# Attention and two expert layers in one kernel: the first float64 weights loaded and decoded in the attention's written order

## The chip, the cores and the metric

The kernel runs on one NeuronCore of a Trainium2 chip: TensorE (matmuls and transposes, called PE in the profile), VectorE (DVE), ScalarE (ACT), GpSimd (POOL) and SyncE (SP, which here only issues transfers) run their own instruction streams and wait for one another by semaphores. The metric is the device time of one execution in microseconds (us).

## The reference

Three parts follow one another. All inputs but the first layer's two weight matrices are float32.

```python
# attention: batch 2, 8 heads, 576 positions, head size 64
q_rot, k_rot = rotate(q), rotate(k)
scores = scale * q_rot @ k_rot.T
attn = exp(scores - max); attn /= sum(attn) + 1e-9
x = (attn @ v) as [1152 tokens, 512]
# first layer: w_in [512, 2048] and w_out [2048, 512] are float64
h = x @ w_in
g = max(h, 0) + log1p(exp(-abs(h)))
x = g @ w_out
# second layer: 8 experts (512 x 1024 x 512); tokens with x @ w_skip > 0 go
# to the expert of the largest logit, weighted by its probability
out = x; out[chosen] += gate * (max(x @ w1[e], 0) @ w2[e])
```

## The kernel before, in words

**Attention.** The work is cut into 40 units: for each batch b and each pair of heads hp five units of query rows, four of 128 rows (for both heads) and one called "m", which holds the last 64 rows of both heads. `Attention.run` goes through the units, i = 0 to 39 and four more steps to finish. In each step it emits instructions in the order that the list `ORDER` gives (line 26): `S0`, `S1` are the scores of the two heads on TensorE (`s_mm`), `M0`, `M1` their row maxima on VectorE (line 249), `E0`, `E1` the exponentials on ScalarE (line 262); `T0` to `T2` are the transposes of the unit before on TensorE (line 331) and `H0` to `H2` the copies of these to SBUF on ScalarE or VectorE (lines 84 and 86). `J` are the value matmuls and `N` the scaling, `Q` prepares the next pair: transposes of rotated queries and keys (`tq`), last keys and queries of all pairs (`tr`, once for each batch), loads, and rotations on GpSimd. `L` calls `do_later`, which takes the low parts that were put off, and issues the transfers that stack keys and queries into both halves of the partitions (`stack`, on SP).

A block `manual_schedule` fixes the order on TensorE, VectorE, ScalarE and SP within one step. What stands outside such a block is placed by a list scheduler, which issues an instruction when its model of the engines finds it ready; `issue_after(x)` adds that an instruction on x's engine is queued behind x.

**Float32 in two halves.** TensorE multiplies rounded float32 (fp32r). A tensor is therefore held as a high part (rounded by a ScalarE copy) and a low part (the rest, a VectorE subtraction), and three products are summed. `halves` emits the high part and returns the low part as a function to be called later.

**First pair.** There is no time to stack, so its scores use keys `kT` and queries `qT` directly with 64 rows. The last 64 keys (positions 512 to 575) of all four pairs are transposed at once by `tr`, rounded into a tile `kr`, and copied from there into the pair's `kT` by `kr_in`.

**Filler matmuls.** `warm(part)` issues `WARM[part]` matmuls on a tile of zeros, at six places of the start: 0 ahead of everything, 1 and 2 behind the first transposes of queries and keys, 3 behind `tr`, 4 behind the first unit's scores, 5 behind unit 1.

**First layer.** `Moe1` takes the hidden dimension in 16 blocks f of 128. A block has two weight halves, (f, 0) of `w_in` and (f, 1) of `w_out`, 512 KB of float64 each. `weights` loads a half on SP as int64 into one of two buffers `raw`, decodes it to float32 by three VectorE integer instructions (lines 540 to 542) into one of two buffers `wt`, rounds it on ScalarE (line 544) and takes the low part on VectorE (line 545). The tokens come in four phases; phase 0 (blocks 0 to 5, the first 512 tokens) begins at the seam with the attention. A step is `hidden` (12 matmuls for these tokens and block, line 557, then softplus on ScalarE and VectorE) and, two steps later, `out_mm` (line 595).

The halves (0, 0), (0, 1), (1, 0), (1, 1) are given out at units 29, 31, 33 and 35 (`W_AT`) by the function `side`, which is called behind the unit's manual block: the load is queued behind the last stack copy so far, the VectorE instructions behind the last maximum so far, and the list scheduler places the rest. The halves (2, 0) and (3, 0) are the first of phase 0's own, outside the attention's loop.

Of the kernel before, what the change touches and what calls it, by code (L numbers as in the profile page):

```python
# [25 lines left out]
ORDER = "S0 R T0 M0 H0 E0 S1 T1 M1 L E1 H1 J T2 N H2 Q".split()  # L26
# [5 lines left out]
W_AT = (29, 31, 33, 35)  # L32

WARM = (18, 4, 4, 3, 3, 3)
# [13 lines left out]
class Attention:  # L48
# [133 lines left out]
    def tr(self, b):  # L182
# [18 lines left out]
    def stack(self, dst, src):  # L201
        for a in range(2):
            r = slice(64 * a, 64 * a + 64)
            for o in range(2):
                d = slice(64 * o, 64 * o + 64)
                self.copied = self.nc.sync.dma_start(dst(a, d).bitcast(F32), src(a, o, r).bitcast(F32))
# [104 lines left out]
    def t_steps(self, b, hp, u):  # L311
# [18 lines left out]
        def tr(ps, i, src):  # L330
            nc.tensor.transpose(ps[:, 128 * i : 128 * i + 128], src, ident)  # L331
# [75 lines left out]
    def run(self, side=None):  # L407
        nc = self.nc
# [6 lines left out]
        with self.tc.manual_schedule(engines=self.engines):  # L415
# [17 lines left out]
        for i in range(n + 4):  # L433
# [4 lines left out]
            with self.tc.manual_schedule(engines=self.engines):  # L438
                for step in ORDER:
# [25 lines left out]
                    elif step == "L":  # L465
                        self.do_later()
# [9 lines left out]
            if side:  # L476
                side(i)
# [32 lines left out]
class Moe1:  # L510
# [4 lines left out]
    def __init__(self, nc, w_in, w_out, xh, xl):  # L515
        self.nc, self.w_in, self.w_out, self.xh, self.xl = nc, w_in, w_out, xh, xl
        self.w = {}

    def weights(self, f, wp, st, bufs, parts=(0, 1), after=nullcontext):
# [4 lines left out]
        w = self.w[f]  # L524
        fs = slice(128 * f, 128 * f + 128)
        for i in parts:
            raw = st.tile([128, 512], mybir.dt.int64, name=f"raw{f}{i}", tag="st", bufs=2)
            if i == 0:
                nc.sync.dma_start(
                    raw.rearrange("p (k n) -> p k n", k=4), self.w_in[:, fs].rearrange("(k p) n -> p k n", p=128)  # L530
                )
            else:
                nc.sync.dma_start(raw, self.w_out[fs, :])
            u = raw.bitcast(U32)
# [699 lines left out]
```

## Time and profile before

| | |
|---|---|
| median of 3 runs | 535.49 us (534.54 to 537.21) |
| profiled execution | 536.5 us |
| its span, first to last instruction | 534.7 us |
| TensorE matmuls busy | 494.9 us (93%) |
| VectorE busy | 396.2 us (74%) |
| ScalarE busy | 342.7 us (64%) |
| GpSimd busy | 121.1 us (23%) |
| mean granted TensorE clock | 0.988 of 2.4 GHz |

The profile is of one execution; times count from its first instruction. A line such as `L557 PE MATMUL h<-xh,w ... x464 | 105.2, 309 | 2.7 <-ACT w L544 1.7` is a group: line of the kernel, engine, operation, output and inputs with their shapes, how many, busy us and mean ns of one, and the engine's idle time just before them with what ended it. In the timeline `x4` means that four instructions of one kind run in one row, and `SPq` is the issue of a transfer on SP. PEld is the loading of the stationary operand. The clock that the chip granted TensorE is 1.00 at 2.4 GHz and 0.50 at 1.2 GHz; a mean between stands for a stretch with both.

### The profile page before, as it was taken

The numbers are of one execution on the slowest core, as the hardware profiler recorded it, in microseconds if no ns is written. First come the engines' busy times: TensorE is split into PE (matmuls) and PEld (weight loads), VectorE is DVE, ScalarE is ACT, GpSimd is POOL, SyncE is SP. The second block draws the span as 40 slices with busy tenths as digits, with TensorE's granted clock in tenths as the row PEclk, the third lists the DMA queues.
The fourth block names the chain that finished last, engine by engine and source line by source line (L and its number), as shares of the span: only waits on it lengthen the run. The fifth ranks groups of instructions, "written<-read, shape, count | busy, mean of one in ns | idle before, by whom it ended". The sixth has DMA issues, their size and how long they took to land. (4 is left out here: it accounts for less than half of the span.)

```text
span 534.7 us, 8595 instructions
## 1 busy us (share of the span) xinstructions
PE 494.9 (93%) x2894; PEld 397.6 (74%) x2895; DVE 396.2 (74%) x734; ACT 342.7 (64%) x770; POOL 121.1 (23%) x165
## 2 busy tenths in 40 slices
PE   7889999998879978999999999999989899999994
PEld 3667677776656656889999998998967577777773
DVE  7467687766679389699999885437875678797883
ACT  2456665665656474897677776766863487676781
POOL 0848675745113210000000000001100502221112
PEclk9899999999899999999999999999998999999998
DMA  7176547446453115134343440502333705597101
GB/s 170 51 189 159 121 122 185 108 107 170 98 157 110 51 40 156 41 119 118 120 119 118 119 119 1 198 0 83 102 118 121 266 13 191 188 364 272 54 21 37
DMA packets 41604, 65.47 MB, mean 122 GB/s; under 512 B 9184, under 2 KB 23776, under 8 KB 41552
## 3 DMA queue, kind: packets, MB, share of 16 engines
q1 hardware_dynamic: 37776, 57.89, 37.2%
q0 software_dynamic: 1440, 4.20, 2.1%
q10 hardware_dynamic: 2336, 2.74, 1.6%
q8 instruction: 26, 0.43, 0.4%
q14 instruction: 26, 0.21, 0.1%
HBM read 67.30 MB, written 7.15 MB: 139 GB/s over the span
## 5 line engine op out<-in xcount | busy, mean ns | idle before, releaser
L557 PE MATMUL h<-xh,w 128*128 128x320 f32 (+2 forms) x464 | 105.2, 309 | 2.7 <-ACT w L544 1.7
L595 PE MATMUL acc<-w,gh 128*128 128x512 f32 x288 | 78.3, 398 | 6.1 <-ACT gh L585 6.1
L557 PEld LDWEIGHTS h<-xh,w 128*128 128x128 f32 x464 | 78.1, 188 | 6.6 <-ACT w L544 2.1
L816 DVE TENSOR_TENSOR ws<-raw,ws 128x1024 fp32r<-128x1024 f32 x59 | 70.0, 1220 | 10.2 <-ACT ws L814 9.9
L557 PE MATMUL h<-xl,w 128*128 128x320 f32 (+2 forms) x232 | 69.7, 308 | 0.0
L249 DVE TENSOR_REDUCE m<-s 128x1 f32<-128x576 f32 x64 | 48.0, 753 | 25.8 <-PE s L240 20.0
L595 PEld LDWEIGHTS acc<-w,gh 128*128 128x128 f32 x288 | 51.6, 188 | 18.1 <-ACT gh L585 9.3
L814 ACT CAST ws<-raw 128x1024 fp32r<-128x1024 f32 x59 | 59.3, 1058 | 4.9 <-DMA raw<-in_moe_w_dram 4.7
L262 ACT ACTIVATE P<-s,m 128x576 f32<-128x576 f32 x64 | 47.7, 747 | 18.2 <-DVE m L249 17.9
L904 PE MATMUL y<-ws,hT 128*128 128x512 f32 x216 | 57.6, 408 | 0.5 <-DVE hT L890 0.2
L84 ACT COPY pt<-t 128x384 f32<-128x384 f32 x60 | 28.0, 480 | 40.4 <-PE t L331 40.4
L240 PE MATMUL s<-ks,qs 128*128 128x288 f32 x224 | 44.2, 320 | 9.9 <-ACT P L262 8.1
L570 ACT ACTIVATE y<-h 128x320 f32<-128x320 f32 (+2 forms) x58 | 25.3, 438 | 37.9 <-PE h L557 35.9
L331 PE MATMUL t<-ct,P 128*128 128x128 f32 x288 | 46.9, 282 | 2.4 <-ACT pt L84 1.4
L904 PEld LDWEIGHTS y<-ws,hT 128*128 128x128 f32 x216 | 39.5, 188 | 11.2 <-issue 1.4
L658 POOL TENSOR_SCALAR sc<-lg 128x2 f32<-128x2 f32 (+1 forms) x3 | 0.9, 291 | 204.1 <-DVE lg L641 204.1
L557 PEld LDWEIGHTS h<-xl,w 128*128 128x128 f32 x232 | 43.3, 188 | 2.0
L240 PEld LDWEIGHTS s<-ks,qs 128*128 128x128 f32 x224 | 32.1, 192 | 15.5 <-ACT P L262 11.4
L595 PE MATMUL acc<-w,gl 128*128 128x512 f32 x144 | 43.2, 391 | 0.0
L331 PEld LDWEIGHTS t<-ct,P 128*128 128x128 f32 x288 | 34.6, 143 | 9.6 <-issue 3.0
L586 DVE TENSOR_TENSOR gl<-r,gh 128x256 fp32r<-128x256 f32 (+2 forms) x42 | 25.8, 614 | 21.0 <-ACT gh L585 20.8
L375 PE MATMUL pv<-pt,vr 128*64 128x256 f32 (+1 forms) x256 | 37.7, 418 | 0.0
(262 smaller groups left out, 945.6 us busy)
## 6 DMA issues: line engine op xcount, KB each, us to landing
raw<-in_moe_w_dram SPq DMA_DIRECT2D x68, 512.0 KB
raw<-in_moe_w_in_dram SPq DMA_DIRECT2D x16, 512.0 KB
raw<-in_moe_w_out_dram SPq DMA_DIRECT2D x16, 512.0 KB
ks<-kT SPq DMA_DIRECT2D x28, 288.0 KB
qs<-qT SPq DMA_DIRECT2D x28, 128.0 KB
wr<-in_moe_w_dram SPq DMA_DIRECT2D x5, 512.0 KB
x2d<-x SPq DMA_DIRECT2D x9, 256.0 KB
xn<-in_q_dram SPq DMA_DIRECT2D x8, 256.0 KB
```

Source lines behind the costliest of these rows:

```text
L84: self.nc.scalar.copy(out, in_)
L240: nc.tensor.matmul(ps[:, c, 0:288], lhsT=qs[:, a, uc], rhs=ks[:, a, x, 288 * c : 288 * c + 288], start=x == 0, stop=x == 1,)
L249: self.last = nc.vector.tensor_reduce(st["m"][:, a : a + 1], st["ps"][a][:, :, 0:288], axis=AX.XY, op=ALU.max, negate=True)
L262: nc.scalar.activation(P[:, 576 * a : 576 * a + 576].rearrange("p (c n) -> p c n", c=2), ps[:, :, 0:288], AF.Exp, bias=m[:, a : a + 1], ac ...
L331: nc.tensor.transpose(ps[:, 128 * i : 128 * i + 128], src, ident)
L375: nc.tensor.matmul(ps[64 * a : 64 * a + 64, 0:n], lhsT=p["vr"][:, a, i, :], rhs=pt[:, 5 * a + i, 0:n], start=False, stop=i == 3, skip_grou ...
L557: nc.tensor.matmul(ps[c][:, 0:m], lhsT=w[:, 0, x, 128 * k : 128 * k + 128], rhs=src[:, k, c0 + m * c : c0 + m * c + m], start=z == 0, stop ...
L586: self.last = nc.vector.tensor_sub(gl, r, gh.bitcast(F32))
L595: nc.tensor.matmul(acc[t], lhsT=g[x][:, 128 * j : 128 * j + 128], rhs=w[:, 1, y, :], start=f == f0 and z == 0, stop=f == f1 and z == 2,)
L814: hi = nc.scalar.copy(w[:, 0], raw)
L816: self.did[T, c] = hi.ins, nc.vector.tensor_sub(w[:, 1], raw, w[:, 0].bitcast(F32)).ins
L904: nc.tensor.matmul(py, lhsT=ht[:, x, o : o + 128], rhs=w[:, y, 512 * j : 512 * j + 512], start=c == 0 and j == 0 and z == 0, stop=c == 3 a ...
```

## The change

- `W_AT` names six halves and the unit of each part of their work: the load at units 20, 23, 28, 31, 34 and 37; the first two decoding instructions (`decode`, z = 0), the third (z = 1), the rounding (`high`) and the low part (`low`) at units of their own. (2, 0) and (3, 0) are loaded and decoded there; their `high` and `low` stay in phase 0. All this is a step `W` of the written order, between `H1` and `J`, inside the manual block; the two `issue_after` of `side` are gone.
- `tr(0, True)` rounds the last keys of the first pair from PSUM into `kT`; the rest of its work (`kr` and the masked queries `qm`, high and low parts) is put off to `do_later`. Before, the high parts were emitted at once.
- `do_later` is called at a step `K`, in front of `H0` and `E0`, in units 1 to 4, and at `L` in the others.
- `WARM` goes from (18, 4, 4, 3, 3, 3) to (15, 4, 4, 3, 6, 3).
- The first hidden step of phase 0 is queued behind the attention's last transpose (`tail`).

```diff
-ORDER = "S0 R T0 M0 H0 E0 S1 T1 M1 L E1 H1 J T2 N H2 Q".split()
+ORDER = "S0 R T0 M0 K H0 E0 S1 T1 M1 L E1 H1 W J T2 N H2 Q".split()
-W_AT = (29, 31, 33, 35)
-WARM = (18, 4, 4, 3, 3, 3)
+W_AT = (
+    ((0, 0), (20, 26, 27, 27, 28)), ((0, 1), (23, 29, 30, 30, 31)), ((1, 0), (28, 32, 33, 33, 34)),
+    ((1, 1), (31, 35, 36, 36, 37)), ((2, 0), (34, 38, 39)), ((3, 0), (37, 40, 41)),
+)
+WARM = (15, 4, 4, 3, 6, 3)
...
-    def tr(self, b):
+    def tr(self, b, first=False):
...
+        if first:
+            kT = self.pr[b, 0]["kT"].rearrange("p x (i c) -> p x i c", c=64)[:, :, 0::9, :]
+            self.halves(kT[:, 0], kT[:, 1], ps[:, 0, 64:128].unsqueeze(1).to_broadcast([128, 2, 64]))()
+        self.later.append(partial(self.tr_in, b, ps))
+
+    def tr_in(self, b, ps):
         kr = self.kr[b] = self.wq.tile([128, 2, NP, 64], F32R, name=f"kr{b}", tag="kr", bufs=1)
-        self.later.append(self.halves(kr[:, 0], kr[:, 1], ps[:, :, 64:128]))
+        self.halves(kr[:, 0], kr[:, 1], ps[:, :, 64:128])()
         qm = self.qm[b]
         for a in range(2):
             r = slice(64 * a, 64 * a + 64)
-            self.later.append(self.halves(qm[r, :, 0, r], qm[r, :, 1, r], ps[r, :, 0:64], True))
+            self.halves(qm[r, :, 0, r], qm[r, :, 1, r], ps[r, :, 0:64], True)()
...
-            nc.tensor.transpose(ps[:, 128 * i : 128 * i + 128], src, ident)
+            self.tail = nc.tensor.transpose(ps[:, 128 * i : 128 * i + 128], src, ident)
...
             low_q, _, low_k, _ = self.later
             self.later = []
-            self.tr(0)
             low_q()
             low_k()
-            self.later.pop(0)()
-            self.kr_in(0, 0, "a")
+            self.tr(0, True)
             self.warm(3)
...
-                    elif step == "L":
-                        self.do_later()
+                    elif step in "KL":
+                        if (step == "K") == (0 < i < 5):
+                            self.do_later()
+                    elif step == "W" and side:
+                        side(i)
...
-            if side:
-                side(i)
...
+    def decode(self, f, x, z):
+        nc = self.nc
+        u = self.raw[f, x].bitcast(U32)
+        lo, hi = u[:, 0::2], u[:, 1::2]
+        if z == 0:
+            self.t[f, x] = self.st.tile([128, 512], F32, name=f"wt{f}{x}", tag="wt", bufs=2)
+        tu = self.t[f, x].bitcast(U32)
+        if z == 0:
+            nc.vector.tensor_scalar(tu, hi, 3, 0x3FFFFFFF, op0=ALU.logical_shift_left, op1=ALU.bitwise_and)
+            nc.vector.scalar_tensor_tensor(tu, hi, 0xC0000000, tu, op0=ALU.bitwise_and, op1=ALU.bitwise_or)
+        else:
+            nc.vector.scalar_tensor_tensor(tu, lo, 29, tu, op0=ALU.logical_shift_right, op1=ALU.bitwise_or)
+    def high(self, f, x, wp, bufs):
+        if f not in self.w:
+            self.w[f] = wp.tile([128, 2, 2, 512], F32R, name=f"w{f}", tag="w", bufs=bufs)
+        self.nc.scalar.copy(self.w[f][:, x, 0, :], self.t[f, x])
+    def low(self, f, x):
+        w = self.w[f][:, x]
+        self.nc.vector.tensor_sub(w[:, 1, :], self.t[f, x], w[:, 0, :].bitcast(F32))
+    def weights(self, f, x, wp, bufs, after):
+        if (f, x) not in self.t:
+            self.load(f, x)
             with after():
...
+                self.decode(f, x, 0)
+                self.decode(f, x, 1)
+        with after():
+            self.high(f, x, wp, bufs)
+            self.low(f, x)
...
             def side(i):
...
+                for (f, x), at in W_AT:
+                    for k, job in enumerate((moe1.load, moe1.decode, moe1.decode, moe1.high, moe1.low)[: len(at)]):
+                        if at[k] == i:
+                            job(f, x, **({"z": k - 1} if 0 < k < 3 else {"wp": wa, "bufs": 2} if k == 3 else {}))
...
                 with ExitStack() as order:
+                    if not pend and ph == 0:
+                        order.enter_context(tc.issue_after(att.tail.ins))
```

## Rows read from the trace of the kernel before

**Rows 1.** The page: busy us, instructions; a group of part 5.

```profile
PE 494.9 (93%) x2894; PEld 397.6 (74%) x2895; DVE 396.2 (74%) x734; ACT 342.7 (64%) x770; POOL 121.1 (23%) x165
...
L84 ACT COPY pt<-t 128x384 f32<-128x384 f32 x60 | 28.0, 480 | 40.4 <-PE t L331 40.4
```

**Rows 2.** By stretch: PE, PEld, DVE, ACT, POOL busy (instructions), clock, DMA.

```profile
20.00:30.00 10.00, 10.00 (x58) 7.60 (x56) 5.12 (x9) 5.76 (x15) 6.01 (x8) 0.83 0.13 27
...
100.20:118.60 18.40, 17.70 (x132) 13.46 (x130) 12.68 (x27) 12.57 (x31) 11.62 (x17) 1.00 0.56 139
118.60:141.10 22.50, 19.16 (x130) 14.53 (x128) 14.72 (x31) 13.10 (x32) 9.37 (x13) 0.92 0.46 115
141.10:163.30 22.20, 18.33 (x128) 13.10 (x126) 17.08 (x34) 12.58 (x31) 4.41 (x7) 1.00 0.67 170
```

**Rows 3.** Line 222, 64-row units: ns min/median/max, first and last start.

```profile
L222 PE MATMUL s10m<-kT,qm x6: 292/296/378, 100.2 to 101.0; 128*128 128x288 f32 x6
L222 PE MATMUL s11m<-kT,qm x6: 291/298/378, 118.6 to 119.3; 128*128 128x288 f32 x6
L222 PE MATMUL s12m<-kT,qm x6: 292/296/378, 141.1 to 141.9; 128*128 128x288 f32 x6
L222 PE MATMUL s13m<-kT,qm x6: 292/296/378, 163.3 to 164.0; 128*128 128x288 f32 x6
```

**Rows 4.** Groups, 130 to 170 us: busy, mean ns, idle before.

```profile
L541 DVE SCALAR_TENSOR_TENSOR wt<-raw,wt 128x512 uint32<-128x512 uint32 x5 | 3.9, 784 | 0.0
L542 DVE SCALAR_TENSOR_TENSOR wt<-raw,wt 128x512 uint32<-128x512 uint32 x5 | 3.4, 681 | 0.0
L545 DVE TENSOR_TENSOR w<-wt,w 128x512 fp32r<-128x512 f32 x4 | 2.7, 680 | 0.0
L540 DVE TENSOR_SCALAR wt<-raw 128x512 uint32<-128x512 uint32 x6 | 2.5, 423 | 5.1 <-DMA raw<-in_moe_w_out_dram 3.0 <-DMA raw<-in_moe_w_in_dram 2.0
```

**Rows 5.** Timeline, 127 to 132 us: start, length, engine [idle before].

```profile
127.89 0.59 SPq L529 DMA_DIRECT2D raw<-in_moe_w_in_dram  x1
...
131.85 0.43 DVE L540 TENSOR_SCALAR wt<-raw 128x512 uint32<-128x512 uint32 x1 [1.96 <-DMA raw<-in_moe_w_in_dram]
```

**Rows 6.** Timeline of the start, 12 to 37 us.

```profile
12.66 0.37 ACT L153 CAST kr<-tr 128x256 fp32r<-128x256 f32 x1 [1.42 <-PE tr L187]
12.93 0.77 ACT L149 ACTIVATE qm<-tr 64x256 fp32r<-64x256 f32 x2
...
14.19 0.41 ACT L84 CAST kT<-kr 128x256 fp32r<-128x256 f32 x1 [0.49 <-DVE kr L427]
14.64 1.30 PE L234 MATMUL s<-kT,qT 64*128 64x288 f32 x11 [1.05 <-ACT kT L84]
...
17.28 1.05 PE L234 MATMUL s<-kT,qT 64*128 64x288 f32 x6 [0.58 <-ACT P L262]
...
24.34 0.76 DVE L249 TENSOR_REDUCE m<-s 128x1 f32<-128x576 f32 x1 [0.85 <-PE s L234]
...
26.59 0.69 DVE L199 TENSOR_TENSOR kT<-tq,kT 128x512 fp32r<-128x512 f32 x1
...
27.34 3.82 SPq L206 DMA_DIRECT2D ks<-kT  x4
...
36.15 0.77 PE L240 MATMUL s<-ks,qs 128*128 128x288 f32 x4 [1.83 <-DMA qs<-qT]
```

**Rows 7.** Timeline of the seam, 175 to 185 us.

```profile
175.19 0.48 PE L557 MATMUL h<-xh,w 128*128 128x512 f32 x1
...
179.61 0.82 PE L331 MATMUL t<-ct,P 128*128 128x128 f32 x6
...
184.81 0.60 ACT L570 ACTIVATE y<-h 128x512 f32<-128x512 f32 x1 [1.52 <-PE t13n L295]
```

**Rows 8.** Timeline, 160 to 162 us.

```profile
160.48 1.29 POOL L387 TENSOR_TENSOR xl<-x,xh 128x256 fp32r<-128x256 f32 x1
...
161.09 1.22 DVE L541 SCALAR_TENSOR_TENSOR wt<-raw,wt 128x512 uint32<-128x512 uint32 x1
```

More of the change, by code (lines that the diff above doesn't have):

```diff
@@ L513, with __init__ @@
     CH = ((0, 512, (0, 1, 2, 3)), (512, 640, (4, 5, 6, 7, 8)), (0, 256, (0, 1)), (256, 256, (2, 3)))
[L515 to L519, printed above, removed]
-        nc = self.nc
+    def __init__(self, nc, w_in, w_out, xh, xl, st):
+        self.nc, self.w_in, self.w_out, self.xh, self.xl, self.st = nc, w_in, w_out, xh, xl, st
+        self.w, self.raw, self.t = {}, {}, {}
@@ new lines, in load @@
+    def load(self, f, x):
+        raw = self.raw[f, x] = self.st.tile([128, 512], mybir.dt.int64, name=f"raw{f}{x}", tag="st", bufs=2)
+        fs = slice(128 * f, 128 * f + 128)
+        if x == 0:
+            src = self.w_in[:, fs].rearrange("(k p) n -> p k n", p=128)
+            self.nc.sync.dma_start(raw.rearrange("p (k n) -> p k n", k=4), src)
+        else:
+            self.nc.sync.dma_start(raw, self.w_out[fs, :])
+    def decode(self, f, x, z):
+        nc = self.nc
+        u = self.raw[f, x].bitcast(U32)
[6 more added lines that the diff above has]
+            nc.vector.scalar_tensor_tensor(tu, hi, 0xC0000000, tu, op0=ALU.bitwise_and, op1=ALU.bitwise_or)
+        else:
+            nc.vector.scalar_tensor_tensor(tu, lo, 29, tu, op0=ALU.logical_shift_right, op1=ALU.bitwise_or)
@@ L522, in weights @@
+    def high(self, f, x, wp, bufs):
         if f not in self.w:
             self.w[f] = wp.tile([128, 2, 2, 512], F32R, name=f"w{f}", tag="w", bufs=bufs)
[L524 to L534, printed above, removed]
-            lo, hi = u[:, 0::2], u[:, 1::2]
-            t = st.tile([128, 512], F32, name=f"wt{f}{i}", tag="wt", bufs=2)
-            tu = t.bitcast(U32)
-            with after():
-                nc.vector.tensor_scalar(tu, hi, 3, 0x3FFFFFFF, op0=ALU.logical_shift_left, op1=ALU.bitwise_and)
-                nc.vector.scalar_tensor_tensor(tu, hi, 0xC0000000, tu, op0=ALU.bitwise_and, op1=ALU.bitwise_or)
-                nc.vector.scalar_tensor_tensor(tu, lo, 29, tu, op0=ALU.logical_shift_right, op1=ALU.bitwise_or)
-                h = w[:, i, 0, :]
-                nc.scalar.copy(h, t)
-                nc.vector.tensor_sub(w[:, i, 1, :], t, h.bitcast(F32))
@@ L1073, in side @@
             def side(i):
-                if i in W_AT:
-                    k = W_AT.index(i)
-                    with tc.issue_after(att.copied.ins):
-                        moe1.weights(k // 2, wa, st, 2, (k % 2,), lambda: tc.issue_after(att.last.ins))
+                for (f, x), at in W_AT:
+                    for k, job in enumerate((moe1.load, moe1.decode, moe1.decode, moe1.high, moe1.low)[: len(at)]):
+                        if at[k] == i:
+                            job(f, x, **({"z": k - 1} if 0 < k < 3 else {"wp": wa, "bufs": 2} if k == 3 else {}))
             att.run(side)
@@ L1138, in attention_moe_moe_kernel @@
                     wb, n = ring[SLOT[fw]]
-                    moe1.weights(fw, wb, st, n, (x,), lambda: tc.issue_after(moe1.last.ins) if pend else nullcontext())
+                    moe1.weights(fw, x, wb, n, lambda: tc.issue_after(moe1.last.ins) if pend else nullcontext())
                 with ExitStack() as order:
+                    if not pend and ph == 0:
+                        order.enter_context(tc.issue_after(att.tail.ins))
                     if (ph, f) > XGT:
```

4 lines of the change are left out of this document (2 added, 2 removed).

## The prediction

> **What bounds the kernel now.** I read the busy shares first: TensorE is busy nine tenths of the span and VectorE three quarters [rows 1], so time can only be won where TensorE stands still or runs at its lower clock. The table by stretches comes next [rows 2]: it compares an undisturbed pair of heads (five units of the attention) with the two pairs in which weight halves are decoded, and the ten microseconds after the start. Then the starts of the 64-row units [rows 3] as a clock of the attention, one per pair. The reader is to see 100.2, 118.6, 141.1 and 163.3: the undisturbed pair takes 18.4 us, the next two 22.5 and 22.2, though TensorE's busy time in them is hardly larger (17.70 against 19.16 and 18.33). So 4.1 + 3.8 = 7.9 us of two pairs are lost, and the groups by line [rows 4] and the timeline [rows 5] say to what: VectorE stood 5.1 us in front of the first decoding instruction, waiting for weights to land, with the maxima and copies of the attention queued behind it. The first half was asked for at 127.89 and decoded at 131.85, some 4.0 us later. The first of these pairs has a mean clock of 0.92 [rows 2], so part of its 4.1 us is TensorE at 1.2 GHz after it had stood.
>
> The start is the second place [rows 6]. TensorE waits at 14.64 for the last keys of the first pair, at 17.28 for the first exponentials, and at 36.15 for the stacked queries of the second pair; between 20 and 30 us the mean clock is 0.83, with TensorE busy all the time [rows 2]. The third place is the seam between attention and first layer [rows 7]: matmuls of the first layer's hidden part begin at 175.19, before the last transposes of the attention, which run only at 179.61; the first activation of that hidden part starts at 184.81, released by the transposes of the attention's last scalings.
>
> **The change part by part.**
>
> *Loads ahead and decoding in the written order.* Loads: none is added. Six stand at units 20, 23, 28, 31, 34 and 37 instead of behind the last stack copy, three to six units ahead of their first decoding. At 18.4 / 5 = 3.7 us a unit that is 11 us or more against the 4.0 us that the load took, so the 5.1 us of VectorE waiting go. A third load needs the buffer of the first: unit 28 comes after the second decoding step at 27, 31 after 30, 34 after 33, 37 after 36, so SP should not stand there. On SP each load is one issue of 0.59 us in front of that unit's other loads and of the next stack copies; the only collision that I see is unit 31, between the key and the query copies of a pair. TensorE would wait if those came late; should a load's whole 4.0 us land in front of the query copies, that is the bound, once. I take nothing, as these copies start some three units before they are read.
>
> Decoding: each half is three VectorE instructions and, for four of the six, a fourth (the low part): 0.42, 0.68, 0.68 and 0.68 us [rows 4] (the mean of 0.784 for L541 holds one slow instance). Six firsts of 0.42 + 0.68, six seconds of 0.68, four lows of 0.68 make 6.6 + 4.1 + 2.7 = 13.4 us, one group in every unit from 26 to 41, 0.84 us a unit. VectorE is busy 12.68 of 18.40 us in the undisturbed pair [rows 2], so 5.7 us are free, against 4.2 us of groups. The place (behind the second copy's step, ahead of the value matmuls) is one where VectorE has little to do until the third transposes; but what is late there delays the scalings, the third copies and the next unit's first maximum, whose exponential TensorE waits for. How much reaches TensorE no row shows, and the bounds are these. Below, nothing: 0.84 us a unit lies in 1.1 us of free time. Above, the nearest row is the pair from 141.1 to 163.3: VectorE was busy 17.08 us, 4.4 more than undisturbed, and the pair lost 3.8 us. If its one wait of 3.0 us for a load [rows 4] cost nothing, the share is 3.8 / 4.4 = 0.86; if it cost its whole length, 0.8 of 4.4, a fifth. I take the fifth, as the wait held up everything behind it: 2.7 us (0 to 11.5). Gain of this part: 7.9 - 2.7 = 5.2 us (-3.6 to 7.9). The second clock drop is inside the 7.9. The four ScalarE roundings are only moved.
>
> A row speaks for a higher price: at 161.09 the second decoding instruction took 1.22 us beside GpSimd's subtraction of 1.29 us [rows 8], against 0.68 elsewhere. The first two halves now stand in units 26 to 31, where GpSimd still rotates the last pair, so six of these instructions could each take 0.54 us longer: 3.2 us of VectorE time, 0.6 us at a fifth. That I leave inside the range. The Trainium skill, "SBUF — State Buffer", section "Who interferes with whom", says that a VectorE instruction with two SBUF inputs contends with a GpSimd instruction that reads SBUF, and that the loser is fully blocked for the other's whole length. The trace agrees as far as 1.22 against 0.68 goes; by the rule each of the six could wait for a whole GpSimd instruction, with the 1.29 us seen here 7.7 us of VectorE time, which at a fifth is 1.5 us instead of 0.6.
>
> *First last-keys.* Before, the last keys of all pairs are rounded (0.37), the queries' high parts follow (0.77), VectorE takes the low part, ScalarE copies both into place, and TensorE goes on at 14.64 [rows 6]. After, ScalarE rounds the first pair's 64 columns from PSUM straight into place and VectorE takes the low part: at most 0.37 from 12.66, then under 0.4, so TensorE can go on near 13.45, 1.2 us earlier. Against that the 1.14 us of ScalarE work for the rest now stands in unit 0 between the two exponentials, and the second is what TensorE needs next. I take 0.6, between 0 and 1.2.
>
> *Later steps ahead.* In units 1 to 4 the low parts and stack copies come before the first exponential's place, not behind the second maximum. The first maximum of unit 2 ends at 24.34 + 0.76 = 25.10; the low part of the keys then stands at 25.10, not 26.59, 1.5 us earlier. SP issues the key copies for 3.82 us from 27.34 and the query copies right behind, so the end at 36.15 moves with that first issue. TensorE idled 1.83 us there, which caps the gain: 1.5 (0 to 1.8). What is late next is TensorE's own work. The second maxima of units 2 and 3 wait for the low parts now; as they stood only 0.7 us from them before, I cost that at nothing, 0.7 us each if it is not hidden.
>
> *Clock-keeping.* Three fewer filler matmuls at the start (the rotation in front of the first transposes is what they wait for), three more behind the first scores, where TensorE idled 0.58 us at 17.28 [rows 6]. If these three are not hidden they cost under 0.48 us each (the 512-column row of [rows 7]), 1.4 us together. What they may give is the 0.17 of 10 us in the clock column [rows 2]: 1.7 us if the drop to 1.2 GHz goes. No row tells which filler prevents it; I take 0.7, between -1.4 and 1.7.
>
> *The seam.* Only the first hidden step is queued behind the attention's last transposes. If TensorE does one hidden step there and not two, these transposes come up to 179.61 - 175.19 = 4.4 us earlier, and the attention's end half of that, 2.2 us, since one hidden step still stands in front of its value matmuls. But the second step isn't held back and can take the freed place: then nothing is won. If neither runs, TensorE idles for two copies of 0.48 us [rows 1]. I take 0.5 (-1.0 to 2.2). Behind the seam nothing is taken away: the first instructions of six halves, not four, stand between 130 and 170 us already [rows 4], so VectorE has the same decoding in phase 0.
>
> **Sum.** 5.2 + 0.6 + 1.5 + 0.7 + 0.5 = 8.5 us off the profiled execution's 536.5 us (span 534.7 and 1.8 around it): 528.0. That execution was 1.0 us above the median of the runs, 535.49, so I expect the changed kernel's median at 527.0. The ends of the terms add up to a gain of 7.9 + 1.2 + 1.8 + 1.7 + 2.2 = 14.8 and a loss of 3.6 + 1.4 + 1.0 = 6.0 (520.7 to 541.5); they don't all fall on one side, so the forecast's own range, with a share of VectorE's up to a third, is 522 to 532.
>
> **Rivals.**
> - *Half of it does nothing*: the second hidden step fills the place of the first, and the clock drops at the start as before. For it: the order names one step only, and three fillers are few. Against: the gap at 17.28 is just what three fillers cover. Then 0.7 and 0.5 fall out: 528.2.
> - *VectorE's written order takes the place of the load's wait*: each group stands in a fixed place in front of a maximum, nothing can be moved past it any more, and it reaches TensorE. With GpSimd's blocking the groups are 13.4 + 3.2 = 16.6 us. If all of it reaches TensorE, the attention is 16.6 - 7.9 = 8.7 us longer, less 3.3 from the other parts: 535.5 + 5.4 = 540.9, slower. It is slower by over 0.5% from a share of (7.9 + 3.3 + 2.7) / 16.6 = 0.84 on, and within 0.5% from about 0.51 on. For it: at 17.08 busy of 22.2 us VectorE already cost something. Against: the free 1.1 us a unit.
> - *Stack copies come late behind the loads*: unit 31's load delays the query copies by up to 4.0 us: 531.0.
>
> **How the numbers follow.** Forecast 0.46, half of it 0.16, late copies 0.08: all faster by over 0.5% (0.5% is about what a measurement of this kernel tells from no change: below 532.8). VectorE's order with a share of 0.51 to 0.84: 0.16, the same; above: 0.14, slower. So 0.70, 0.16, 0.14. The range: 521.5, a little beyond the forecast's low end as both clock and seam may give all, to 536, within the rival of VectorE's order.
>
> **What would show it.** Right: the starts of the 64-row units of the last two pairs some 19 to 20 us apart; no wait of VectorE for weights before unit 41; the scores of the second pair some 2.8 us earlier than 36.15; the clock column at 20 to 30 us at 1.00 for the clock term; the last unit's transposes ahead of the first hidden matmul for the seam. Wrong: waits of TensorE for exponentials grown beside decoding instructions, decoding instructions of over 1 us, hidden matmuls still ahead of the last transposes, or time given back in the first layer, where nothing is taken away.

## The result, and the profile after

The changed kernel takes 528.74 us (median of four executions, 527.75 to 537.05) against 536.35 us of the kernel before on the same chip (four, 534.54 to 538.13): ratio 0.9852, 95% interval 0.9803 to 0.9901. The forecast was 527.0, in a range of 521.5 to 536.0. The ratio leaves out the execution at 537.05, whose mean granted clock was 0.969 against 0.99 in the other three, while the median counts it, and so it is with every run below. The profiled execution took 527.75 us; its span is 525.8, which is 8.9 less than before.

The work is the same (by the page TensorE is busy 493.2 us against 494.9 and VectorE 397.6 against 396.2); what went is time in which TensorE stood or ran at half clock. Where it went is read from the 64-row units of each pair (first and last start at the end of a row), as [rows 3]:

```profile
L232 PE MATMUL s02m<-kT,qm x6: 288/294/377, 67.7 to 68.4; 128*128 128x288 f32 x6
L232 PE MATMUL s03m<-kT,qm x6: 291/298/378, 88.2 to 89.0; 128*128 128x288 f32 x6
L232 PE MATMUL s10m<-kT,qm x6: 292/296/378, 98.5 to 99.2; 128*128 128x288 f32 x6
L232 PE MATMUL s11m<-kT,qm x6: 288/294/377, 116.8 to 117.5; 128*128 128x288 f32 x6
L232 PE MATMUL s12m<-kT,qm x6: 292/296/378, 136.2 to 137.0; 128*128 128x288 f32 x6
L232 PE MATMUL s13m<-kT,qm x6: 288/294/377, 155.3 to 156.0; 128*128 128x288 f32 x6
```

Two rows of before that are not among [rows 3] belong beside the first two:

```profile
L222 PE MATMUL s02m<-kT,qm x6: 291/297/378, 70.7 to 71.4; 128*128 128x288 f32 x6
L222 PE MATMUL s03m<-kT,qm x6: 291/298/378, 90.0 to 90.7; 128*128 128x288 f32 x6
```

| stretch, us | before | after | won |
|---|---|---|---|
| start to the second pair's first stacked scores | 36.15 | 33.15 | 3.0 |
| pair s02m to s03m | 19.3 | 20.5 | -1.2 |
| undisturbed pair s10m to s11m | 18.4 | 18.3 | 0.1 |
| pair s11m to s12m | 22.5 | 19.4 | 3.1 |
| pair s12m to s13m | 22.2 | 19.1 | 3.1 |
| s13m to the end of the last scalings' transposes (t13n) | 21.6 | 20.2 | 1.4 |
| from there to the end | 349.8 | 350.3 | -0.5 |

The two stretches that the table leaves out (the stacked scores to s02m, and s03m to s10m) are as long as before within 0.1 us. Rounded to tenths the lines make 9.0, the span says 8.9. The last line goes with a later and longer drop of the clock near 400 us, in code that the change does not touch (granted 0.83 between 390 and 410 us; before 0.91 between 400 and 420).

The stretches of after, with the columns of [rows 2]:

```profile
20.00:30.00 10.00, 10.00 (x69) 7.42 (x67) 5.85 (x11) 5.86 (x15) 8.52 (x10) 1.00 0.46 100
98.50:116.80 18.30, 17.59 (x131) 13.35 (x129) 12.85 (x27) 12.56 (x31) 11.57 (x16) 1.00 0.56 140
116.80:136.20 19.40, 17.81 (x130) 13.38 (x129) 17.34 (x34) 13.41 (x33) 9.77 (x12) 1.00 0.53 131
136.20:155.30 19.10, 16.98 (x128) 13.18 (x126) 15.74 (x36) 12.71 (x32) 3.80 (x8) 1.00 0.61 145
```

All clocks are at 1.00. The third busy time of a row is VectorE's: 17.34 and 15.74 us in the two decoding pairs against 12.85 undisturbed, 4.5 + 2.9 = 7.4 us more. The decoding instructions in the two pairs take 5.4 + 4.4 = 9.8 us; VectorE's other work is lighter there. The pairs are 1.1 + 0.8 = 1.9 us longer than the undisturbed one, about a quarter of the 7.4 us and a fifth of the 9.8. Not all of that is VectorE's: in the second of these pairs TensorE waits 0.75 us for the stacked queries of the last pair, whose copies SP issues behind the load of unit 31:

```profile
139.15 1.35 SPq L536 DMA_DIRECT2D raw<-in_moe_w_out_dram  x1
...
147.88 0.77 PE L250 MATMUL s<-ks,qs 128*128 128x288 f32 x4 [0.75 <-DMA qs<-qT]
```

Before, the same load stood in the same place (143.42), in a pair that was longer, and TensorE did not wait for these queries.

The decoding groups as [rows 4], from 116 to 172 us. VectorE's idle time in front of the first instruction of a half was 5.1 us before and is gone:

```profile
L550 DVE SCALAR_TENSOR_TENSOR wt<-raw,wt 128x512 uint32<-128x512 uint32 x6 | 5.3, 886 | 0.1
...
L547 DVE TENSOR_SCALAR wt<-raw 128x512 uint32<-128x512 uint32 x6 | 2.8, 468 | 0.0
```

Issues of the loads, as [rows 5]. The first two stand at 14 us, not in units 20 and 23; their buffers were free and nothing on SP held them there:

```profile
13.78 0.47 SPq L534 DMA_DIRECT2D raw<-in_moe_w_in_dram  x1
14.29 0.50 SPq L536 DMA_DIRECT2D raw<-in_moe_w_out_dram  x1
```

The start, as [rows 6]:

```profile
12.91 1.44 PE L244 MATMUL s<-kT,qT 64*128 64x288 f32 x12
...
18.52 1.05 PE L244 MATMUL s<-kT,qT 64*128 64x288 f32 x6 [1.30 <-ACT P L272]
...
22.65 0.76 DVE L259 TENSOR_REDUCE m<-s 128x1 f32<-128x576 f32 x1 [0.82 <-PE s L244]
...
23.44 0.69 DVE L209 TENSOR_TENSOR kT<-tq,kT 128x512 fp32r<-128x512 f32 x1
...
24.20 3.84 SPq L216 DMA_DIRECT2D ks<-kT  x4
...
33.15 0.77 PE L250 MATMUL s<-ks,qs 128*128 128x288 f32 x4 [0.52 <-DMA qs<-qT]
```

The wait in front of 14.64 is gone, and twelve of the first scores run from 12.91. The low part of the keys follows the first maximum at once (23.44 behind 22.65 + 0.76) and the copies go out at 24.20. TensorE now waits 1.30 us at 18.52 for the second exponential of the first unit.

The pair that became longer, s02m to s03m. ScalarE, VectorE and again ScalarE wait for one another on the second batch's last queries (1.53 us here, 0.61 us once more at 75.67), and TensorE 2.09 us for the end of it:

```profile
74.68 0.38 ACT L153 ACTIVATE qm<-tr 64x256 fp32r<-64x256 f32 x1 [1.53 <-DVE kr L200]
...
76.56 0.55 PE L341 MATMUL t<-ct,P 128*128 128x128 f32 x3 [2.09 <-DVE qm L204]
```

The seam, as [rows 7]. The last transposes come first now, ahead of all hidden matmuls; yet 20 hidden matmuls (one step of 12 and most of the next) still stand in front of the value matmuls at 172.01; before it was 24:

```profile
165.90 1.69 PE L341 MATMUL t<-ct,P 128*128 128x128 f32 x12
...
167.34 0.48 PE L581 MATMUL h<-xh,w 128*128 128x512 f32 x1
...
172.01 0.70 PE L382 MATMUL pv<-pt,vd 128*128 128x320 f32 x2
...
174.94 0.55 PE L305 MATMUL t13n<-ct,R 128*128 128x128 f32 x3
```

And a decoding instruction beside the last rotations, as [rows 8], with GpSimd's instructions one by one:

```profile
120.21 1.27 POOL L126 TENSOR_TENSOR rot<-xn,cr 128x512 f32<-128x512 f32 x1
...
120.57 1.46 DVE L550 SCALAR_TENSOR_TENSOR wt<-raw,wt 128x512 uint32<-128x512 uint32 x1
...
121.44 1.73 POOL L129 TENSOR_TENSOR rot<-rot,rt 128x512 f32<-128x512 f32 x1
```

The rotation that was running when VectorE's instruction began kept its length (1.27 us, like the one before it); VectorE's ends at 122.03, 0.55 us behind the end of that rotation, and the rotation that follows takes 1.73 us instead of 1.27.

### The profile page after: what moved, and what is told of

Read it like the earlier page. It is cut to its first block, busy times and chain, and to the rows that moved or that the text cites. A ratio compares the mean times of both kernels' runs of the same rounds, so it can differ in the third digit from the quotient of the medians.

```text
span 525.8 us, 8591 instructions
## 1 busy us (share of the span) xinstructions
PE 493.2 (94%) x2895; PEld 395.9 (75%) x2895; DVE 397.6 (76%) x735; ACT 341.8 (65%) x770; POOL 118.8 (23%) x165
## 5 line engine op out<-in xcount | busy, mean ns | idle before, releaser
L928 PE MATMUL y<-ws,hT 128*128 128x512 f32 x216 | 59.8, 415 | 0.9 <-DVE ws L840 0.2
L272 ACT ACTIVATE P<-s,m 128x576 f32<-128x576 f32 x64 | 47.7, 749 | 12.9 <-DVE m L259 12.8
L341 PE MATMUL t<-ct,P 128*128 128x128 f32 x288 | 45.5, 277 | 3.7 <-DVE qm L204 2.1
```

The source lines that it names most:

```text
L272: nc.scalar.activation(P[:, 576 * a : 576 * a + 576].rearrange("p (c n) -> p c n", c=2), ps[:, :, 0:288], AF.Exp, bias=m[:, a : a + 1], ac ...
L341: self.tail = nc.tensor.transpose(ps[:, 128 * i : 128 * i + 128], src, ident)
L928: nc.tensor.matmul(py, lhsT=ht[:, x, o : o + 128], rhs=w[:, y, 512 * j : 512 * j + 512], start=c == 0 and j == 0 and z == 0, stop=c == 3 a ...
```

## The experiments

The theory: in the attention the early landing of the weights is what won the time, and VectorE has room for the decoding. Its main rival: the written places won it. Each run is the changed kernel with one edit; medians stand beside those of the kernel before on the same chip.

**e1. Loads as changed, decoding unordered.** The places of the decoding are left to the list scheduler: a half is decoded, rounded and its low part taken behind the block of the unit that held its first decoding instruction.

```diff
-                    for k, job in enumerate((moe1.load, moe1.decode, moe1.decode, moe1.high, moe1.low)[: len(at)]):
...
+                    if at[0] == i:
+                        moe1.load(f, x)
...
+                    if at[1] == i:
+                        with tc.issue_after(att.last.ins):
+                            moe1.decode(f, x, 0)
+                            moe1.decode(f, x, 1)
+                            if len(at) > 3:
+                                moe1.high(f, x, wa, 2)
+                                moe1.low(f, x)
```

> The changed kernel with its loads where they are, but each half's decoding, rounding and low part given out whole behind the unit's block, placed by the list scheduler as in the kernel before. Theory 1 (the attention's gain of some 6 us came from weights that land before they are decoded): the starts of the 64-row units stay 19 to 20 us apart in the last two pairs, as in the changed kernel (19.4 and 19.1), and the time stays within 1.5 us of it. Theory 2 (the written places of the decoding made the gain): the two pairs go back to 21 us or more each and the time rises by 3 to 6 us.

530.97 us (before 536.84), ratio 0.9886 (0.9844 to 0.9928). The pairs by its 64-row units:

```profile
L232 PE MATMUL s11m<-kT,qm x6: 291/298/378, 118.1 to 118.9; 128*128 128x288 f32 x6
L232 PE MATMUL s12m<-kT,qm x6: 288/294/377, 137.9 to 138.6; 128*128 128x288 f32 x6
L232 PE MATMUL s13m<-kT,qm x6: 288/294/377, 156.8 to 157.5; 128*128 128x288 f32 x6
```

19.8 and 18.9 us, 38.7 together against 38.5 with written places and 44.7 before: the whole gain of the two pairs is there without the written order. The median is 2.2 us above the changed kernel's, more than the 1.5 expected. Of that the trace shows two pieces: from s13m to the end of t13n it takes 21.4 us against 20.2, and this execution had the clock drop at its start (below).

**e2. Places as changed, loads late.** Each load goes out in the unit of its first decoding, behind the last stack copy.

```diff
+                    if at[1] == i:
+                        with tc.issue_after(att.copied.ins):
+                            moe1.load(f, x)
```

> The changed kernel with each of the six loads at the unit of its first decoding instruction, behind the last stack copy, and the decoding at its written places. Theory 1 (landing): VectorE stands 2 to 4 us in front of each first decoding instruction, the last two pairs take 22 to 26 us each, and the time rises by 8 to 16 us, past the kernel before. Theory 2 (places): the pairs stay under 20.5 us and the time within 2 us.

545.92 us (before 536.84), ratio 1.0175 (1.0144 to 1.0206): slower than the kernel before, which had late loads too. The pairs take 29.4 and 27.4 us, more than the 22 to 26 expected. Its waits from 112 to 180 us (in total, times, longest):

```profile
DVE wt L547 <- DMA raw<-in_moe_w_in_dram: 9.5, 2, 6.8
...
PE t10n L305 <- POOL R L92: 9.3, 1, 9.3
```

So the two parts depend on each other: the two pairs together take 44.7 us with late loads and free places (the kernel before, which differs in more than this), 38.7 with early loads and free places, 38.5 with both early and written, and 56.8 with late loads in written places. In a written order a load that is late holds up every step behind it (the reciprocal, GpSimd's row of scalings, the transposes of them on TensorE); in the kernel before, where the scheduler chose the places, 5.1 us of such waits cost 7.9. Early loads are what wins, and what makes the written order harmless.

**e3. Decoding twice.** The three decoding instructions run a second time: 6 x (0.42 + 0.68 + 0.68) = 10.7 us more on VectorE by [rows 4].

```diff
                         if at[k] == i:
+                            for _ in range(2 if 0 < k < 3 else 1):
...
```

> The changed kernel with each decoding instruction of the six halves in the attention issued twice (the result is the same): 6 x (0.42 + 0.68 + 0.68) = 10.7 us more for VectorE in units 26 to 41. It prices VectorE's time in the written order. If a fifth of it reaches TensorE, as the prediction took: 2 us longer. If all of it does: 11 us longer, as the rival of VectorE's order has it. If VectorE has room for none: within 0.5 us.

545.92 us (before 536.84), ratio 1.0189 (1.0159 to 1.0219), some 17 us above the changed kernel for 10.7 us of work, and more than the 11 us of the dearest case expected. The two pairs by stretches:

```profile
116.97:142.35 25.38, 19.68 (x127) 14.85 (x125) 20.67 (x38) 13.27 (x32) 10.07 (x12) 0.87 0.41 100
142.35:167.34 24.99, 21.04 (x131) 15.04 (x130) 19.64 (x41) 13.07 (x33) 3.81 (x7) 0.86 0.43 111
```

VectorE's busy time grew by 3.3 + 3.9 = 7.2 us, the pairs by 6.0 + 5.9 = 11.9. Of these at most 25.38 x 0.13 + 24.99 x 0.14 = 6.8 us are the clock's (TensorE at 1.2 GHz after it had stood). What it stood for, first of all:

```profile
120.27 1.23 DVE L293 TENSOR_SCALAR sm<-sm 128x5 f32<-128x5 f32 x1
...
123.14 1.32 DVE L550 SCALAR_TENSOR_TENSOR wt<-raw,wt 128x512 uint32<-128x512 uint32 x1
...
124.39 0.17 DVE L294 RECIPROCAL sm<-sm 128x5 f32<-128x5 f32 x1
124.65 1.07 POOL L92 TENSOR_SCALAR R<-sm 128x256 f32<-128x256 f32 x2 [0.74 <-DVE sm L294]
...
125.51 0.90 PE L305 MATMUL t10n<-ct,R 128*128 128x128 f32 x3 [4.67 <-POOL R L92]
```

A reciprocal of 0.17 us stands behind decoding, GpSimd's scalings behind it, and TensorE 4.67 us behind these. The second long wait is for the stacked queries of the last pair again: 2.77 us at 154.87, 0.75 in the changed kernel. The room on VectorE is real, but it is not a constant share of what is put there: the first 7.4 us made the pairs longer by a quarter of their length or less, the next 7.2 by more than their whole, the clock included.

**e4. The second batch's last queries as before.** For b = 1 the high parts are given out in a row and the low parts behind them, as in the kernel before; the changed kernel alternates.

```diff
-        self.later.append(partial(self.tr_in, b, ps))
+        if first:
+            self.later.append(partial(self.tr_in, b, ps))
+            return
+        kr = self.kr[b] = self.wq.tile([128, 2, NP, 64], F32R, name=f"kr{b}", tag="kr", bufs=1)
+        self.later.append(self.halves(kr[:, 0], kr[:, 1], ps[:, :, 64:128]))
...
+            self.later.append(self.halves(qm[r, :, 0, r], qm[r, :, 1, r], ps[r, :, 0:64], True))
```

> The changed kernel, but the last keys and queries of the second batch are taken as before: the high parts on ScalarE at once, the low parts put off. Theory: in the changed kernel ScalarE and VectorE take turns on one PSUM tile (high, low, high, low, high, low) in unit 15, and the transposes wait 2.09 us for its bank instead of 1.00; so this wait goes back to 1.0 us and the pair from 67.7 to 88.2 (20.5 us) back to 19.4, 1.1 us less in all. Rival (the 1.2 us that this pair lost came from the earlier start meeting GpSimd's rotations): the pair stays at 20.5 us.

527.59 us (before 536.84), ratio 0.9845 (0.9801 to 0.9889). The runs alone don't tell it from the changed kernel; the trace does: the pair s02m to s03m is 19.3 us again and the wait at its place 1.00 instead of 2.09. The alternation costs 1.2 us here. In two other profiles (without step K, and with the first last-keys as before, both below) the granted clock falls to 0.50 right behind this wait of 2.10 us, and the pair takes 22.1 and 22.2 us at a mean clock of 0.92. None of the five profiles with the wait of 1.00 has that drop; of the nine with 2.09 to 2.10 these two have it.

**e5. The seam's order taken out.**

```diff
-                    if not pend and ph == 0:
-                        order.enter_context(tc.issue_after(att.tail.ins))
```

> The changed kernel without the order that queues the first hidden step behind the attention's last transposes. In the changed kernel the stretch from the last 64-row unit to the end of the last scalings' transposes took 20.2 us, before 21.6, and 20 hidden matmuls still stand ahead of the last value matmuls. Theory 1 (the order made this 1.4 us): the hidden matmuls stand ahead of the last transposes again and the stretch goes back to 21.4 or more. Theory 2 (the lighter VectorE made it): the stretch stays within 0.3 us of 20.2 and the time within 0.5 us.

529.89 us (before 536.7), ratio 0.9839 (0.9808 to 0.9871): by the runs no difference. In the trace the last transposes are split again, the second half of them behind hidden matmuls:

```profile
168.13 0.82 PE L341 MATMUL t<-ct,P 128*128 128x128 f32 x6
...
173.37 0.82 PE L341 MATMUL t<-ct,P 128*128 128x128 f32 x6
```

From s13m (157.5) to the end of t13n (178.44) it takes 20.9 us against 20.2, between the two cases expected: the order wins 0.7. The other profiles with this order and each half decoded once, at its written places, take 20.2 us too, all within 0.1.

**e6. The fillers of before.**

```diff
-WARM = (15, 4, 4, 3, 6, 3)
+WARM = (18, 4, 4, 3, 3, 3)
```

> The changed kernel with the fillers of before (18, 4, 4, 3, 3, 3). Theory 1 (fillers keep the clock): the clock falls to 1.2 GHz near 20 us in the profile, as before, and the third unit's scores start 1.4 to 1.7 us later than 21.56. Theory 2 (where the clock falls at the start hangs on the execution, since the changed kernel's front showed no drop in two profiles and a drop at 18.7 to 20.6 us in three): no fixed effect; without a drop the third unit's scores start within 0.2 us of 21.56, with one within 0.3 us of the 22.7 to 23.0 of the changed front.

531.8 us (ten executions, 527.87 to 537.98; before 536.7), ratio 0.9907 (0.9873 to 0.9941). The profile has no drop of the clock at the start, with the fillers of before:

```profile
17.00:25.00 8.00, 6.70 (x44) 5.11 (x45) 4.96 (x9) 5.34 (x14) 7.11 (x9) 1.00 0.32 100
```

The same stretch of the kernel before, and of the run with the second batch's queries as before, which has the new fillers and the drop all the same:

```profile
17.00:25.00 8.00, 7.72 (x39) 5.71 (x40) 3.64 (x8) 4.13 (x12) 7.22 (x9) 0.79 0.01 2
```

```profile
17.00:25.00 8.00, 6.70 (x32) 4.66 (x32) 3.43 (x7) 4.24 (x11) 7.13 (x9) 0.79 0.29 100
```

So the fillers don't decide whether it falls: of the fourteen profiles of kernels with nearly this start (all that are told of here) six have a drop of some 0.21 x 8 / 0.5 = 3.4 us at 1.2 GHz there and eight have none, with either set of fillers in both groups. The six are the kernel before and five of the nine in which TensorE waits 1.30 us for the second exponential near 18.5; the four without that wait (e8 and the three versions at the end) have none. So that wait, which the change itself brought, may be what lets the clock fall; four profiles are too few to show it, and the kernel before has the drop without it. Where the clock falls the second pair's stacked scores start at 34.5 to 35.2 (34.83 in the run just shown), without it at 33.1 to 33.4 (33.35 here) in the kernels that have step K and not the step P of the last versions: about 1.5 us. Whether the fillers make it rarer one profile can't say; the last run below bears on it.

**e7. No step K.**

```diff
-                        if (step == "K") == (0 < i < 5):
+                        if step == "L":
```

> The changed kernel with the low parts and stack copies always at the later step L. From the first maximum of unit 2 to the first stacked scores the kernel before took 11.81 us, the changed one 10.50. Theory (the step ahead made it): back to 11.5 or more, the stacked scores 1.0 to 1.5 us later than with the step, the time 1 us longer. Rival (the distance is set by SP's issue of the copies or by TensorE): 10.5 within 0.3.

533.26 us (ten executions; before 536.7), ratio 0.9936 (0.9908 to 0.9965).

```profile
27.32 3.80 SPq L216 DMA_DIRECT2D ks<-kT  x4
...
36.28 0.87 PE L250 MATMUL s<-ks,qs 128*128 128x288 f32 x4 [1.99 <-DMA qs<-qT]
```

The low part of the keys is back behind the second maximum (it starts at 26.56) and the wait for the stacked queries is 1.99 us. From the first maximum of unit 2 to the stacked scores it takes 11.98 us against 10.50 with the step; from the key copies' issue on it is 8.96 and 8.95. The step wins 1.4 to 1.5 us in the trace. The runs say more (about 4.5 us on 528.7), with granted clocks of 0.978 to 0.987 in most of them. The profiled execution, whose span is 5.4 us longer than the changed kernel's, says what most of the rest is: it has the drop near 20 us (about 1.5 us) and the drop behind the wait of 2.10 us in the pair s02m to s03m (1.6 us). Whether leaving out the step makes these drops more frequent is not settled.

**e8. The first last-keys as before.** The whole of `tr(0)` is given out with its high parts, and the first pair's keys come from `kr`.

```diff
-            self.tr(0, True)
...
+            self.tr(0, True)
...
+            self.later.pop(0)()
+            self.kr_in(0, 0, "a")
```

> The changed kernel with the first last-keys taken as before (all rounded, low part, copy into place). The first unit's scores end 1.3 us later. The prediction's theory: 0.6 us is left of that at the second unit's second scores (18.52 in the changed kernel, so 19.1). Rival (the work put off delays the second exponential from 17.12 to 17.63 and gives it back): 18.7 or less there, so that the edit is worth 0.2 us or nothing.

528.92 us (before 536.7), ratio 0.9838 (0.9813 to 0.9862): no difference.

```profile
18.64 1.06 PE L249 MATMUL s<-kT,qT 64*128 64x288 f32 x6
...
33.08 0.77 PE L255 MATMUL s<-ks,qs 128*128 128x288 f32 x4 [0.49 <-DMA qs<-qT]
```

The wait of 1.05 us for the first pair's last keys is back (at 14.55), yet the second scores start at 18.64 against 18.52 and the stacked ones at 33.08 against 33.15. What the rounding in place wins, the wait of 1.30 us at 18.52 takes back: part of the rest of the work on the last keys (0.36 + 0.38 us on ScalarE, and 0.49 us of its waiting for VectorE's low part between them) stands between the two exponentials.

**The changed kernel once more, and two versions of it, b1 and b2.** b1 gives the rest of that work a step P behind the second exponential of unit 0, with the high parts in a row for both batches; b2 also spreads the halves over units 8 to 39.

> The changed kernel once more, beside the two versions that follow: 527 to 530 us. Whether its profile shows the drop of the clock near 20 us is open; with a drop the third unit's scores start 22.7 to 23.2, without one near 21.6.

```diff
-ORDER = "S0 R T0 M0 K H0 E0 S1 T1 M1 L E1 H1 W J T2 N H2 Q".split()
+ORDER = "S0 R T0 M0 K H0 E0 S1 T1 M1 L E1 P H1 W J T2 N H2 Q".split()
...
-                        if (step == "K") == (0 < i < 5):
+                        if step == ("P" if i == 0 else "K" if i < 5 else "L"):
```

> The changed kernel with the second batch's last keys and queries as before (high parts at once), and the first batch's put-off part behind the second exponential of unit 0, high parts in a row. Theory: the wait of 1.30 us in front of the second unit's second scores (put-off work between the two exponentials) falls below 0.5 and the wait of 2.1 us near 75 us to 1.0: 1.2 us from the pair around 75 us, 0.5 to 1.2 us from the start, 1.7 to 2.4 us in all against the changed kernel. Rival for the start: the second pair's transposes wait for GpSimd's rotation and the start wins nothing, 1.2 us in all.

```diff
-    ((0, 0), (20, 26, 27, 27, 28)), ((0, 1), (23, 29, 30, 30, 31)), ((1, 0), (28, 32, 33, 33, 34)),
+    ((0, 0), (3, 8, 9, 9, 10)), ((0, 1), (3, 18, 19, 19, 20)), ((1, 0), (13, 23, 24, 24, 25)),
...
```

> As the version before, with the six halves spread over units 8 to 39, five units and more each, away from the units in which GpSimd rotates. Theory (VectorE's share grows steeply with how much is decoded in a pair, since decoding twice cost 17 us for 10.7): the pairs from 116.8 on, 19.45 and 18.7 to 19.05 us in the changed kernel against 18.3 undisturbed, come to 18.9 or less, and the pairs before lose less than that: 0.5 to 1 us faster than the version before, and no decoding instruction in the attention over 1 us. Rival (a fixed cost for each decoding instruction, wherever it stands): the same time within 0.3 us.

On one chip, with before at 535.35: the changed kernel 528.56 (0.9844, 0.9799 to 0.9888), b1 525.27 (0.9797, 0.9766 to 0.9828), b2 526.25 (0.9832, 0.9801 to 0.9863). b1 is the fastest by its median and by its trace (span 523.9 against 525.8 and 525.5 of the changed kernel's two profiles); by the ratios it is 2.5 us ahead, but the two intervals overlap. Its rows say where:

```profile
17.48 1.06 PE L254 MATMUL s<-kT,qT 64*128 64x288 f32 x6
...
32.18 0.77 PE L260 MATMUL s<-ks,qs 128*128 128x288 f32 x4 [0.74 <-DMA qs<-qT]
...
74.55 0.55 PE L351 MATMUL t<-ct,P 128*128 128x128 f32 x3 [1.00 <-DVE qm L219]
```

The second scores start 1.04 us earlier and the stacked ones 0.97, so the rounding in place wins when the rest is out of the way. b2 was expected 0.5 to 1 us ahead of b1 and is not. It has the shorter pairs that the room on VectorE promised (18.7, 18.7, 17.8; no load stands in front of the last query copies any more, and the wait for them is gone) and loses it in an earlier pair of 12.9 us against 10.3: two decoding instructions stand in front of a reciprocal (87.25), GpSimd's scalings stand behind it and behind a rotation that waits 3.20 us for its input, and TensorE stands 2.66 us.

```profile
87.25 0.18 DVE L304 RECIPROCAL sm<-sm 128x4 f32<-128x4 f32 x1
...
89.32 0.87 POOL L127 TENSOR_TENSOR rt<-xn,cr 128x256 f32<-128x256 f32 x1 [3.20 <-DMA xn<-in_k_dram]
...
92.65 0.44 PE L315 MATMUL t03n<-ct,R 128*128 128x128 f32 x2 [2.66 <-POOL R L92]
```

**b3. b1 with the fillers of before.** The same edit of `WARM` as above.

> The b1 version with the fillers of the kernel before (18, 4, 4, 3, 3, 3). What is open: one profile with the old fillers on the changed kernel showed no drop of the clock at the start, but its ten runs lay between 527.9 and 538.0 us with mean granted clocks from 0.994 down to 0.970, a median some 3 us above that of the changed kernel. The b1 version's six runs lay within 523.5 to 525.7, so a difference can be told here. Theory 'fillers do nothing': median 525.3, ratio 0.980, clocks of all runs 0.990 or above, stacked scores of the second pair at 32.2. Rival 'fillers make the drop rarer': a median of 526.5 or more, some runs with a mean clock of 0.985 or less.

526.78 us (five executions, 526.53 to 529.14; before 537.02), ratio 0.981 (0.9785 to 0.9836), granted clocks 0.984 to 0.991. It falls just on the rival's side of the line drawn by its median, but that line was drawn for another chip; by the ratios the two differ by 0.0013, some 0.7 us, and the intervals overlap almost whole. On the changed kernel the same edit made 0.9907 of 0.9852, some 3 us, with intervals that overlap too. It stays open whether the fillers do something.

## Why the prediction was right

The total was right (a span 8.9 us shorter for 8.5 forecast), and its largest term for the reason given. That the total came so close is luck in part: the decoding pairs (1.0 us better than forecast), the clock (0.8) and the stretch behind s13m (0.9) made up for the first last-keys (0.6 worse), the second batch's last queries (1.2) and the later clock drop (0.5).

- *Loads ahead and decoding.* Forecast 5.2 us (7.9 lost, less 2.7). The two pairs won 6.2: of the 7.9 that they lost before, 1.9 are left, 0.75 of them a wait for query copies. The share was taken on VectorE's additional busy time (4.4 us in the pair of before, in which the decoding instructions took 6.6) and laid on the decoding time itself, all 13.4 us of it; by the first measure 1.9 of 7.4 us were left, by the second 1.9 of the 9.8 that stand in these two pairs. That a fifth fits so well is therefore partly chance. The unordered run shows that the landing of the loads is the cause, the late-load run that the written places alone win nothing in these pairs.
- *Where the loads stand.* "Six stand at units 20, 23, ..." was wrong for the first two, which went out at 14 us. The written order fixes a place within its unit; it holds nothing back that could go before. No harm came of it. The feared collision at unit 31 did show, in small: the load went out between the key and the query copies, and TensorE waited 0.75 us for these. The term was put at nothing, with 4.0 us as its bound.
- *GpSimd beside decoding.* Forecast up to 0.54 us longer for six instructions. Of the six in units 26 to 31 one did, 1.46 us against 0.68; in a later half one took 1.12 beside GpSimd's subtraction. These two are the 1.2 us by which the six of L550 (mean 0.886) exceed 0.68, against 3.2 forecast. The rule of the Trainium skill, "SBUF — State Buffer", section "Who interferes with whom", by which one of two such instructions is blocked until the other has finished, agrees with the rows: the running rotation kept 1.27 us, VectorE's instruction ended 0.55 us behind it, and the next rotation, which began in between, took 0.46 us longer. With decoding twice even a VectorE instruction with one tensor input, on 128x5 elements, took 1.23 us (0.17 elsewhere) and ended at 121.50, with GpSimd's rotation at 121.47. What the forecast had wrong is how many of the six would meet a GpSimd instruction.
- *Later steps ahead.* 1.5 forecast, 1.4 to 1.5 measured.
- *The seam.* 0.5 forecast, 0.7 measured by taking the order out; of the 1.4 us won behind s13m that is half. The unordered run loses 1.2 us there, which speaks for decoding in fixed places as the rest; what the lighter VectorE does there was not taken apart. The hidden matmuls did take the place before the value matmuls, as feared.
- *First last-keys: failed.* "0.6, between 0 and 1.2": it won nothing. The price, ScalarE work between the two exponentials, was seen, and half of the gain was set against it; with the waiting for VectorE's low part it took the whole.
- *Clock-keeping: inside its range, cause not shown.* The clock column reads 1.00 at 20 to 30 us, as forecast for the case that the fillers work. But the run with the old fillers has no drop either, and five with the new ones have it. The 3.0 us won at the start are the step K (1.4) and a drop that did not fall in this execution (about 1.5); the latter is luck as far as is known.
- *Missed: the second batch's last queries,* 1.2 us lost. The diff wraps the work in `tr_in`, where `halves(...)()` gives out high, low, high, low, and before it was high, high, high and then the lows. The prediction read that only for the first batch.
- *The rivals.* "VectorE's written order" gave a constant share to VectorE's time. Such a share does not exist: 0.25 or less for the first 7.4 us and about 1.65 (11.9 / 7.2) for the next. Its point of decision, 0.84, was to be sought in the amount of work, not in a share. "Late stack copies" occurred with 0.75 of its 4.0 us. "Half of it does nothing" (528.2) is as near to the measured medians as the forecast (527.0), and the time can't tell the two apart; the trace shows the seam to win 0.7 and leaves the fillers open.

## What to carry to other kernels

A load that lands before the step that reads it lets a fixed order be written at little price (here at most 1.9 us in two pairs); a late one makes every step behind it late, so move the loads first and the work second. Look also at what stands behind the load in its queue: here query copies, and a wait of 0.75 us. Free time of an off-path engine is not a budget that can be spent to its end: look at which short instruction (here a reciprocal of 0.17 us) stands behind the added work and how many queues follow from it. When a diff wraps emitting code into a new function, write down the order of emission per engine before and after, for every caller.

## What was not expected of the hardware

- High and low parts that are taken in turn from one PSUM tile cost time: with high, low, high, low parts ScalarE waited 1.53 and 0.61 us for VectorE's low parts and TensorE 2.09 us, against 1.00 with the high parts in a row. The first low part stood behind a maximum in VectorE's queue (it runs from 74.23 to 74.65, ScalarE goes on at 74.68). Why a high part waits for the low part of another tile was not tried.
- A wait of TensorE does not always cost the same: behind the same wait of 2.10 us the granted clock fell to 0.50 in two of nine profiles, and the pair then took 22.1 and 22.2 us instead of 20.5.
- The drop of the granted clock to 1.2 GHz near 19 to 20 us falls in six of fourteen profiles of kernels with nearly the same start, and is worth about 1.5 us. None of the runs shows what prevents it.
